# Attention scores issued two query tiles ahead, and a head's value products in two runs instead of four

## The chip, the cores and the metric

The kernel runs on one core of one Trainium2 chip. The metric is device time in microseconds (us) of one execution. The engines named below are TensorE (PE in the profile, with its weight loads as PEld), VectorE (DVE), ScalarE (ACT), GpSimd (POOL) and SyncE (SP), which issues most DMAs. Each works through its own queue in order; semaphores hold an instruction until what it needs is there.

## The reference

Three stages follow one another. The change touches only the first, an attention in which a query sees only the keys of its own hash bucket; its output goes through a routed mixture of experts and a gated feed-forward block.

```python
q_bits = (np.einsum('bhsd,dk->bhsk', q, proj) > 0); k_bits likewise   # 6 bits: a bucket
mask = q_bucket[:, :, :, None] == k_bucket[:, :, None, :]
scores = scale * np.matmul(q, k.transpose(0, 1, 3, 2))                # 2 x 8 heads, 768 x 768, head size 64
scores = np.where(mask, scores, -1000000000.0)
scores = scores - np.max(scores, axis=-1, keepdims=True)
attn = np.exp(scores)
attn = attn / (np.sum(attn, axis=-1, keepdims=True) + 1e-09)
return np.matmul(attn, v)
```

## The kernel before

The attention stage handles 16 heads (2 batches of 8) one after another, and each head in 6 query tiles of 128 rows. One loop over g counts all 96 tiles: head h = g // 6, tile t = g % 6. In this text "t0" to "t5" are the six passes of that loop for one head. A pass does this for its tile:

- `scores(g)` (L151): four matmuls on PE, two with 76 rows (64 of the head, 12 of the hash code) and two with the low parts of the split operands, into one of two buffers in PSUM (`ps_s`, `bufs=2`).
- `smax(g)` (L161): DVE reduces the 768 scores of each row (`mm`, L164), then a tiny scalar_tensor_tensor with two operands in SBUF makes scale and bias (`sb`, L165).
- `sexp(g)` (L170): ACT takes the exponential of the PSUM scores into `p`, with the row sum (L172, a second small instruction reads the accumulator).
- `tposes(g, half)` (L178): three PE transposes of 128x128 (L185) per half, each half then copied from PSUM by ACT (L189) or DVE (L191) into `PT`.

Other work is placed between these. For the head before, `av_step(h - 1, k)` (L195) makes the value product of key tile k with stationary operands 64 columns wide, two side by side (L200). For two heads before, `o_evac` and `o_out` (L217, L228) copy, scale and project the result. For the next head, `hash_mm(h + 1)` (L123, stationary operands 32 columns wide) and `hash_codes` (L140) make the hash code on DVE, and four small SP DMAs write it into the operands of the scores (L147). For the head after that, `split_a` (L100, ACT) and `split_b` (L107) split queries and keys into high and low parts: the query's low part on DVE (L115) beside a POOL copy (L116), the key's low part and copy both on POOL (L118, L119). `load(h + 3)` starts the input DMAs.

Everything is written out by hand (`tc.manual_schedule()`): each engine executes in the order in which the Python calls come. Before the change, pass g issues the scores of tile g + 1, then the value products or hash (list `early`), then the transposes of tile g, while the place of the exponential of tile g + 1 among the PSUM copies is set per pass by `K['se']`. `side(pos)` (L733) issues the exponential and the splits before, between and after the two halves of the transposes. `AV_AT` says which value products stand in which pass.

Of the kernel before, what the change touches and what calls it, by code (L numbers as in the profile page):

```python
# [21 lines left out]
N, DM, E, FF, F2 = 1536, 512, 8, 1024, 1536  # L22
C = 224
GR = ((0, 6), (6, 4), (10, 2))
K = {'se': (0, 1, 2, 1, 1, 2), 'ev': (0, 0, 0, 1, 0, 1, 0, 0, 0, 1, 0, 0), 'avl': (), 'oul': 0, 'hml': 0, 'hc': ((0, 0), (0, 2), (1, 1), (2, 1)), 'sa': ((2, 2), (4, 1)), 'sb': ((3, 2), (4, 2)), 'ext': (1, 0, 2, 4, 7, 8), 'hm0': 0, 'hc0': ((1, 0), (1, 2), (3, 0), (4, 1))}
C_ID, C_TRI, C_THR, C_REV, C_TOK, C_IOTA, C_BASE, C_SLOT = 0, 128, 256, 258, 266, 278, 279, 287
CW = C_SLOT + C
FAR = 1024.0
AV_AT = {1: (0, 1), 2: (2,), 3: (3, 4), 5: (5,)}


@with_exitstack
def attn_moe_kernel(ctx: ExitStack, tc: tile.TileContext, xin, cst, projd, wblk, wmoe, w2in, out):
# [54 lines left out]
    NHD = NB * NH  # L88
# [34 lines left out]
    def hash_mm(h, order=range(4)):  # L123
        p = (ps_m if h or 2 in order else ps_a).tile([128, 512], F32, tag="m" if h or 2 in order else "a", name="m")
        for j in order:
            i = j // 2
            hp_[h, j] = p
            PE.matmul(
                p[32 * j:32 * j + 32, :384], pst[:, 32 * i:32 * i + 32], X[h][:, j * 384:(j + 1) * 384],
                start=True, stop=True, skip_group_check=True,  # L130
            )
# [19 lines left out]
    def scores(g):  # L151
        h, t = divmod(g, NT)
        p = ps_s.tile([128, 2, 512], F32, tag="s", name="s")
        st[g] = p
        qs = slice(t * 128, t * 128 + 128)
        for c in range(2):
            sl = slice(c * 384, c * 384 + 384)
            PE.matmul(p[:, c, :384], T[h, 0][:76, qs], T[h, 1][:76, sl], start=True, stop=False)  # L158
            PE.matmul(p[:, c, :384], B[h, 0][:, qs], B[h, 1][:, sl], start=False, stop=True)  # L159

    def smax(g):  # L161
        m = mm[:, g % 4]
        sb = sm.tile([128, 2], F32, tag="sb", name="sb")
        DVE.tensor_reduce(out=m[:, 1:2], in_=st[g][:, :, :384], axis=AX.XY, op=ALU.min)  # L164
        DVE.scalar_tensor_tensor(  # L165
            out=sb, in0=m[:, 1:2].to_broadcast([128, 2]), scalar=BIG / 2, in1=m, op0=ALU.is_le, op1=ALU.mult
        )
        scl[g], nbs[g] = sb[:, 0:1], sb[:, 1:2]
# [26 lines left out]
    def av_step(h, k):  # L195
        if k == 0:
            av[h] = ps_a.tile([128, 512], F32, tag="a", name="av")
        v = V[h][:, k]
        for c in range(2):
            PE.matmul(  # L200
                av[h][c * 64:(c + 1) * 64, :384], v, PT[h][:, k, c * 384:(c + 1) * 384],
                start=(k == 0), stop=(k == NT - 1), skip_group_check=True,
            )
# [13 lines left out]
    def o_evac(h, q=None, copy=DVE.tensor_copy):  # L217
        n = q[1] * 128 if q else 384
        o = sm.tile([128, n], F32, tag="o" if q is None else f"o{n}", name="o", bufs=2 if q is None else 1)
        copy(o, av.pop((h, q) if q else h)[:, :n])  # L220
        oT[h, q] = o
        t0, nt = q or (0, NT)
        r = sm.tile([128, NT], F32, tag="r", name="r", bufs=2)
        DVE.tensor_reduce(out=r[:, :nt], in_=sums[:, h * 6 + t0:h * 6 + t0 + nt], axis=AX.X, op=ALU.add)
        DVE.reciprocal(r[:, :nt], r[:, :nt])
        rs[h, q] = r

    def o_out(h, q=None):  # L228
        b, hh = divmod(h, NH)
        o, r = oT.pop((h, q)), rs.pop((h, q))  # L230
        p = ps_m.tile([128, 512], F32, tag="m", name="m")
        t0, nt = q or (0, NT)
        t = slice(b * 6 + t0, b * 6 + t0 + nt)
        lp = sm.tile([128, nt, 16], F32, tag=f"lp{nt}", name="lp", bufs=2) if hh else lg[:, t]
        xo = x_all[:, t, hh * 64:(hh + 1) * 64]
        if q is None:
            for j in range(3):
                PE.matmul(p[:, j * 160:(j + 1) * 160], o[:, j * 128:(j + 1) * 128], wb[:, hh], start=True, stop=True)
            ps = p[:, :480].rearrange("p (j c n) -> p j c n", j=3, c=2)
            rr = r.rearrange("p (c j) -> p j c", c=2).unsqueeze(3)  # L240
            lo, xo, sh = lp.rearrange("p (c j) n -> p j c n", c=2), xo.rearrange("p (c j) n -> p j c n", c=2), [128, 3, 2]
        else:
            for j in range(nt):
                PE.matmul(p[:, j * 80:(j + 1) * 80], o[:, j * 128:(j + 1) * 128], wl, start=True, stop=True)
            ps = p[:, :nt * 80].rearrange("p (j n) -> p j n", j=nt)
            rr, lo, sh = r[:, :nt].unsqueeze(2), lp, [128, nt]
        DVE.tensor_tensor(out=lo, in0=ps[..., 64:], in1=rr.to_broadcast(sh + [16]), op=ALU.mult)
        DVE.tensor_tensor(out=xo, in0=ps[..., :64], in1=rr.to_broadcast(sh + [64]), op=ALU.mult)
        if hh:
            (DVE if hh >= NH - 2 else POOL).tensor_tensor(out=lg[:, t], in0=lg[:, t], in1=lp, op=ALU.add)  # L250
# [344 lines left out]
    with tc.manual_schedule():  # L595
# [72 lines left out]
        L = NHD - 1  # L668
# [6 lines left out]
        qa, qb = (0, 4), (4, 2)  # L675
        for g in range(NG):
            h, t = divmod(g, NT)
            if t == 1 and h + 3 < NHD:
                load(h + 3)
            if g + 1 < NG:  # L680
                scores(g + 1)
                smax(g + 1)
            if g < NT:
                set_up(g)
            if 2 * NT <= g < 2 * NT + (E * C + N) // 256:
                for i in (g - 2 * NT,):
                    nc.sync.dma_start(
                        out=xr[i * 256:(i + 1) * 256].rearrange("(p r) d -> p r d", p=128),
                        in_=zeros[0].unsqueeze(1).to_broadcast([128, 2, 512]),
                    )  # L690
            if g == 6 * NT:
                for n in range(4):
                    for part in range(2):
                        w_load(n, part)
            if g == 10 * NT + 1:
                r = router(0)
                todo = [r["s1"], r["s1b"], None, lambda: (r["s2"](), r["s2c"]()), r["s2b"], r["s4"], r["s4b"]]
                for f in r["sc"]:
                    todo += [f, None]
                todo += [r["s4c"], r["s3"], r["s5"]]  # L700
            early, late = [], []
            if h < L:
                if h:
                    for k in AV_AT.get(t, ()):
                        early.append(lambda k=k: av_step(h - 1, k))
                if h > 1 and t == 4:
                    (late if K["oul"] else early).append(lambda: o_out(h - 2))
                if t == (0 if h else K["hm0"]):
                    (late if K["hml"] else early).append(lambda: hash_mm(h + 1))
            elif t < 3:  # L710
                av_step(h - 1, 2 * t)
                av_step(h - 1, 2 * t + 1)
                if t == 0:
                    o_out(h - 2)
                if t == 2:
                    o_evac(h - 1)
            elif t == 3:
                o_out(h - 1)
            else:
                k = 3 * (t - 4)  # L720
                av_group(h, qa, (k, k + 1, k + 2))
                if t == 5:
                    o_evac(h, qa)
            for f in early:
                f()
            if h and h < L and t == 5 and not K["avl"].count(5):
                o_evac(h - 1)
            if g > 10 * NT + 1 and todo:
                f = todo.pop(0)
                if f:  # L730
                    f()

            def side(pos):  # L733
                if g + 1 < NG and K["se"][t] == pos:
                    sexp(g + 1)
                for i in range(2):
                    if h + 2 < NHD and K["sa"][i] == (t, pos):
                        split_a(h + 2, i)
                    if h + 2 < NHD and K["sb"][i] == (t, pos):
                        split_b(h + 2, i)  # L740
                if h < L and (t, pos) == (1, 0):
                    hash_codes(h + 1)

            side(0)
            tposes(g, 0)
            side(1)
            tposes(g, 1)
            for f in late:
                f()
            if h and h < L and t == 5 and K["avl"].count(5):  # L750
                o_evac(h - 1)
            side(2)
            for f in extra.get((h - L + 1, t), ()):
                f()
# [578 lines left out]
```

## Time and profile before

| | before |
|---|---|
| median of 3 runs | 748.94 us (748.5 to 750.65) |
| the profiled execution's own time | 749.55 us |
| its span, first to last instruction | 747.7 us |
| PE busy | 728.7 us (97%) |
| DVE busy | 527.3 us (71%) |
| ACT busy | 434.4 us (58%) |
| POOL busy | 279.4 us (37%) |
| granted PE clock | full speed over nearly the whole span |

The busy shares are means over all three stages. The attention stage takes roughly the first 260 us of the span. PE time is modelled at the end of each matmul, so successive matmuls overlap in the records; the start times tell the pace.

### The profile page before, as it was taken

The numbers are of one execution on the slowest core, as the hardware profiler recorded it, in microseconds if no ns is written. First come the engines' busy times: TensorE is split into PE (matmuls) and PEld (weight loads), VectorE is DVE, ScalarE is ACT, GpSimd is POOL, SyncE is SP. The second block draws the span as 40 slices with busy tenths as digits, with TensorE's granted clock in tenths as the row PEclk, the third lists the DMA queues.
The fourth block names the chain that finished last, engine by engine and source line by source line (L and its number), as shares of the span: only waits on it lengthen the run. The fifth ranks groups of instructions, "written<-read, shape, count | busy, mean of one in ns | idle before, by whom it ended". The sixth has DMA issues, their size and how long they took to land.

```text
span 747.7 us, 13437 instructions
## 1 busy us (share of the span) xinstructions
PE 728.7 (97%) x4621; PEld 617.5 (83%) x4622; DVE 527.3 (71%) x1033; ACT 434.4 (58%) x945; POOL 279.4 (37%) x319
## 2 busy tenths in 40 slices
PE   8899999999999999999999999999999999999995
PEld 6666666666666699999999999999999988999984
DVE  6787777778787777778779876778676245756641
ACT  6777777777777546666677744444554334344331
POOL 3222232322434265122111123444434466565543
PEclk9999999999999999999999999999999999999998
DMA  7367251221302038788897754545463332212202
GB/s 237 116 225 262 77 172 58 71 98 61 114 33 61 15 110 287 225 192 235 267 339 227 221 159 151 219 162 215 165 214 116 111 101 69 85 47 81 58 1 88
DMA packets 49594, 107.37 MB, mean 144 GB/s; under 512 B 8096, under 2 KB 11504, under 8 KB 47984
## 3 DMA queue, kind: packets, MB, share of 16 engines
q1 hardware_dynamic: 46848, 99.94, 41.4%
q0 software_dynamic: 2304, 6.31, 2.3%
q8 instruction: 38, 0.62, 0.4%
q14 instruction: 36, 0.29, 0.1%
q10 hardware_dynamic: 368, 0.20, 0.1%
HBM read 82.76 MB, written 22.56 MB: 141 GB/s over the span
## 4 chain that ended last, share of the span: by engine, by line
PE 80%; DVE 8%; ACT 5%; issue 4%; POOL 1%; DMA 1%; SPq 0%; DVEq 0%; POOLq 0%; ACTq 0%
PE tp L185 8%; PE av L200 8%; PE y L934 5%; PE acc L1056 4%; PE acc L1055 4%; PE acc L1057 4%; PE h L896 3%; PE h L895 3%; PE h L894 3%; PE s L158 3%; PE s L159 3%; ACT p L172 3%; PE y L935 3%; DVE mm L164 2%; PE abb L894 2%
## 5 line engine op out<-in xcount | busy, mean ns | idle before, releaser
L164 DVE TENSOR_REDUCE mm<-s 128x1 f32<-128x768 f32 x96 | 91.8, 956 | 31.5 <-PE s L159 27.1
L185 PEld LDWEIGHTS tp<-cs,p 128*128 128x128 f32 x576 | 62.1, 140 | 55.3 <-ACT p L172 35.9
L853 POOL TENSOR_TENSOR pc<-t,pc 128x256 fp32r<-128x256 f32 x86 | 74.8, 893 | 84.1 <-ACT pc L852 84.1
L172 ACT ACTIVATE p<-s,sb 128x768 f32<-128x768 f32 x96 | 95.0, 989 | 15.9 <-PE tp L185 8.9
L189 ACT ACTIVATE pt<-tp 128x384 f32<-128x384 f32 x144 | 67.0, 489 | 45.5 <-PE tp L185 44.3
L185 PE MATMUL tp<-cs,p 128*128 128x128 f32 x576 | 83.4, 281 | 6.8 <-ACT p L172 5.1
L478 DVE TENSOR_TENSOR wl<-wr,wh 128x512 fp32r<-128x512 f32 x125 | 81.0, 688 | 8.3 <-ACT wh L477 3.5
L477 ACT ACTIVATE wh<-wr 128x512 fp32r<-128x512 f32 x128 | 73.7, 624 | 4.0 <-DMA wr<-wmoe 3.9
L934 PE MATMUL y<-hl,wh 128*128 128x448 f32 x224 | 74.9, 378 | 0.2
L158 PE MATMUL s<-tk,tq 76*128 76x384 f32 x192 | 73.1, 381 | 0.3 <-DVE tq L135 0.3
L894 PE MATMUL h<-xh,wh 128*128 128x224 f32 x256 | 71.4, 279 | 0.2 <-ACT xh L411 0.2
L200 PE MATMUL av<-pt,v 128*64 128x384 f32 x360 | 71.1, 503 | 0.0
L896 PE MATMUL h<-xh,wl 128*128 128x224 f32 x256 | 70.6, 276 | 0.2 <-DVE wl L478 0.2
L895 PE MATMUL h<-xl,wh 128*128 128x224 f32 x256 | 70.2, 274 | 0.3 <-DVE xl L412 0.3
L159 PE MATMUL s<-bk,bq 128*128 128x384 f32 x192 | 65.0, 339 | 0.0
L935 PE MATMUL y<-hl,wl 128*128 128x224 f32 x224 | 59.5, 266 | 0.0
L1055 PE MATMUL acc<-h,gh 128*128 128x512 f32 x144 | 56.7, 394 | 0.4 <-ACT gh L1041 0.4
L1056 PE MATMUL acc<-l,gh 128*128 128x512 f32 x144 | 56.8, 395 | 0.0
L1057 PE MATMUL acc<-h,gl 128*128 128x512 f32 x144 | 56.7, 394 | 0.0
L865 POOL TENSOR_TENSOR l<-t,h 128x512 fp32r<-128x512 f32 x24 | 31.0, 1292 | 64.7 <-ACT h L864 64.7
L116 POOL CAST bq<-tq 64x768 fp32r<-64x768 f32 x15 | 19.3, 1288 | 89.3 <-ACT tq L103 87.4
L907 ACT ACTIVATE hl<-h 128x224 fp32r<-128x224 f32 x64 | 22.8, 356 | 47.6 <-PE h L896 46.8
(225 smaller groups left out, 1889.9 us busy)
## 6 DMA issues: line engine op xcount, KB each, us to landing
wr<-wmoe SPq DMA_DIRECT2D x128, 256.0 KB
r<-w2in SPq DMA_DIRECT2D x12, 1536.0 KB
x<-xin SPq DMA_DIRECT2D x30, 384.0 KB
w<-t SPq DMA_DIRECT2D x36, 256.0 KB
t<-w SPq DMA_DIRECT2D x36, 256.0 KB
xr<-zero SPq DMA_DIRECT2D x13, 512.0 KB
xg<-xr SPq DMA_DIRECT2D x14, 256.0 KB
v<-xin SPq DMA_DIRECT2D x16, 192.0 KB
```

The source lines that it names most:

```text
L158: PE.matmul(p[:, c, :384], T[h, 0][:76, qs], T[h, 1][:76, sl], start=True, stop=False)
L159: PE.matmul(p[:, c, :384], B[h, 0][:, qs], B[h, 1][:, sl], start=False, stop=True)
L164: DVE.tensor_reduce(out=m[:, 1:2], in_=st[g][:, :, :384], axis=AX.XY, op=ALU.min)
L172: ACT.activation(p.rearrange("p (c n) -> p c n", c=2), st.pop(g)[:, :, :384], ACTF.Exp, scale=scl.pop(g), bias=nbs.pop(g), accum_out=sums[ ...
L185: PE.transpose(ps[:, j * 128:(j + 1) * 128], pt_[g][:, k * 128:(k + 1) * 128], ident)
L200: PE.matmul(av[h][c * 64:(c + 1) * 64, :384], v, PT[h][:, k, c * 384:(c + 1) * 384], start=(k == 0), stop=(k == NT - 1), skip_group_check= ...
L894: PE.matmul(ps, wh, xh, start=first, stop=False)
L895: PE.matmul(ps, wh, xl, start=False, stop=False)
L896: PE.matmul(ps, wl, xh, start=False, stop=last)
L934: PE.matmul(p, wh[:, w], hl, start=(f == 0), stop=False, skip_group_check=True)
L1055: PE.matmul(acc[i], h[:, w], wh, start=(f == 0), stop=False)
L1056: PE.matmul(acc[i], h[:, w], wl, start=False, stop=False)
```

## The change

Three things change in the attention loop. Pass g issues the scores of tile g + 2 instead of g + 1 (the first pass issues both). The exponential of tile g + 1 always comes first on ACT, before the PSUM copies of the pass. The value products of a head stand in two runs of three key tiles, after the transposes of t1 and t4 (list `late`), instead of four runs of two, one, two and one before the transposes of t1, t2, t3 and t5. With them move the hash (t0 to t1, now behind the transposes and directly ahead of a run of value products), `o_out` (t4 to t3), `o_evac` (t5 to t4), the input load (t1 to t2) and the splits of queries and keys, for heads from the second on: ACT parts after t1 and t4, DVE and POOL parts after t2 and t5.

```diff
-K = {'se': (0, 1, 2, 1, 1, 2), ..., 'sa': ((2, 2), (4, 1)), 'sb': ((3, 2), (4, 2)), ..., 'hm0': 0, ...}
+K = {'se': (0, 0, 0, 0, 0, 0), ..., 'sa': ((1, 2), (4, 2)), 'sb': ((2, 2), (5, 2)), 'sa0': ((2, 2), (4, 1)), 'sb0': ((3, 2), (4, 2)), ...}
...
-AV_AT = {1: (0, 1), 2: (2,), 3: (3, 4), 5: (5,)}
+AV_AT = {1: (0, 1, 2), 4: (3, 4, 5)}
...
-            if t == 1 and h + 3 < NHD:
+            if t == 2 and h + 3 < NHD:
                 load(h + 3)
-            if g + 1 < NG:
-                scores(g + 1)
-                smax(g + 1)
+            for k in (g + 1, g + 2) if g == 0 else (g + 2,):
+                if k < NG:
+                    scores(k)
+                    smax(k)
...
             if h < L:
+                if t == (1 if h else 0):
+                    (late if h else early).append(lambda: hash_mm(h + 1))
+                    if h:
+                        late.append(lambda: hash_codes(h + 1))
                 if h:
                     for k in AV_AT.get(t, ()):
-                        early.append(lambda k=k: av_step(h - 1, k))
-                if h > 1 and t == 4:
-                    (late if K["oul"] else early).append(lambda: o_out(h - 2))
-                if t == (0 if h else K["hm0"]):
-                    (late if K["hml"] else early).append(lambda: hash_mm(h + 1))
-            elif t < 3:
-                av_step(h - 1, 2 * t)
-                av_step(h - 1, 2 * t + 1)
+                        late.append(lambda k=k: av_step(h - 1, k))
+                if h > 1 and t == 3:
+                    early.append(lambda: o_out(h - 2))
+            elif t < 2:
                 if t == 0:
                     o_out(h - 2)
-                if t == 2:
-                    o_evac(h - 1)
+                for k in range(3 * t, 3 * t + 3):
+                    late.append(lambda k=k: av_step(h - 1, k))
+                if t:
+                    late.append(lambda: o_evac(h - 1))
             elif t == 3:
                 o_out(h - 1)
-            else:
+            if h == L and t > 3:
                 k = 3 * (t - 4)
-                av_group(h, qa, (k, k + 1, k + 2))
+                late.append(lambda: av_group(h, qa, (k, k + 1, k + 2)))
                 if t == 5:
-                    o_evac(h, qa)
+                    late.append(lambda: o_evac(h, qa))
+            if h and t == 4 and h < L:
+                late.append(lambda: o_evac(h - 1))
             for f in early:
                 f()
-            if h and h < L and t == 5 and not K["avl"].count(5):
-                o_evac(h - 1)
...
-                    if h + 2 < NHD and K["sa"][i] == (t, pos):
+                    if h + 2 < NHD and K["sa" if h else "sa0"][i] == (t, pos):
                         split_a(h + 2, i)
-                    if h + 2 < NHD and K["sb"][i] == (t, pos):
+                    if h + 2 < NHD and K["sb" if h else "sb0"][i] == (t, pos):
                         split_b(h + 2, i)
-                if h < L and (t, pos) == (1, 0):
+                if (g, pos) == (1, 0):
                     hash_codes(h + 1)
```

## Rows read from the trace of the kernel before

**Rows 1.** Busy time by stretch: us, PE, PEld, DVE, ACT, POOL; PEclk, DMA share, GB/s.

```profile
100.00:125.00 25.00, 24.76 (x163) 15.79 (x161) 18.41 (x36) 18.61 (x38) 7.26 (x6) 1.00 0.34 119
...
110.00:111.00 1.00, 1.00 (x10) 0.92 (x9) 0.89 (x1) 0.34 (x1) 1.00 (x1) 1.00 0.00 0
```

**Rows 2.** Timeline of PE, one head (t0 to t5): start us, us, engine, line, tile.

```profile
100.01 0.42 PE L158 MATMUL s<-tk,tq 76*128 76x384 f32 x1
...
100.89 0.85 PE L128 MATMUL m<-x,pst 128*32 128x384 f32 x8
...
101.86 0.88 PE L185 MATMUL tp<-cs,p 128*128 128x128 f32 x6
...
102.50 0.42 PE L158 MATMUL s<-tk,tq 76*128 76x384 f32 x1
...
103.38 1.51 PE L200 MATMUL av<-pt,v 128*64 128x384 f32 x8
...
104.82 0.88 PE L185 MATMUL tp<-cs,p 128*128 128x128 f32 x6
...
105.45 0.42 PE L158 MATMUL s<-tk,tq 76*128 76x384 f32 x1
...
107.76 0.42 PE L158 MATMUL s<-tk,tq 76*128 76x384 f32 x1
...
110.71 0.42 PE L158 MATMUL s<-tk,tq 76*128 76x384 f32 x1
...
111.50 0.98 PE L238 MATMUL m<-wb,o 128*128 128x160 f32 x6
...
112.89 0.42 PE L158 MATMUL s<-tk,tq 76*128 76x384 f32 x1
...
115.21 0.42 PE L158 MATMUL s<-tk,tq 76*128 76x384 f32 x1
```

**Rows 3.** Timeline of PE, last head: value products directly behind transposes.

```profile
253.05 0.88 PE L185 MATMUL tp<-cs,p 128*128 128x128 f32 x6
253.85 1.93 PE L210 MATMUL av<-pt,v 128*64 128x512 f32 x6
```

**Rows 4.** Timeline of DVE and ACT: from scores to exponential.

```profile
100.72 0.99 ACT L172 ACTIVATE p<-s,sb 128x768 f32<-128x768 f32 x1
...
101.00 0.96 DVE L164 TENSOR_REDUCE mm<-s 128x1 f32<-128x768 f32 x1 [0.39 <-PE s L159]
...
117.18 0.20 DVE L165 SCALAR_TENSOR_TENSOR sb<-mm 128x2 f32<-128x2 f32 x1
...
117.50 0.99 ACT L172 ACTIVATE p<-s,sb 128x768 f32<-128x768 f32 x1 [0.50 <-DVE sb L165]
```

**Rows 5.** Timeline of POOL, DVE and ACT around the key splits.

```profile
99.00 0.84 ACT L103 ACTIVATE tk<-x 128x768 fp32r<-128x768 f32 x1
...
99.98 1.83 POOL L118 TENSOR_TENSOR bk<-x,tk 64x768 fp32r<-64x768 f32 x1 [1.60 <-issue]
...
101.86 0.82 POOL L119 CAST bk<-tk 64x768 fp32r<-64x768 f32 x1
101.99 0.71 DVE L165 SCALAR_TENSOR_TENSOR sb<-mm 128x2 f32<-128x2 f32 x1
```

**Rows 6.** Timeline of ACT and DVE: the copies, the query's low part, an undisturbed sb.

```profile
103.80 0.86 ACT L189 ACTIVATE pt<-tp 128x384 f32<-128x384 f32 x2
...
109.81 0.16 DVE L165 SCALAR_TENSOR_TENSOR sb<-mm 128x2 f32<-128x2 f32 x1
109.94 0.95 DVE L115 SCALAR_TENSOR_TENSOR bq<-x,tq 64x768 fp32r<-64x768 f32 x1
...
113.41 0.55 DVE L191 COPY pt<-tp 128x384 f32<-128x384 f32 x1
```

**Rows 7.** Timeline of SP: the last two DMAs of a hash code.

```profile
107.37 1.47 SPq L147 DMA_DIRECT2D tk<-code  x2
```

**Rows 8.** Waits of PE from 30 to 250 us: us in all, times, longest.

```profile
PE tp L185 <- ACT p L172: 1.5, 2, 1.0
```

More of the change, by code (lines that the diff above doesn't have):

```diff
@@ L24 @@
 GR = ((0, 6), (6, 4), (10, 2))
-K = {'se': (0, 1, 2, 1, 1, 2), 'ev': (0, 0, 0, 1, 0, 1, 0, 0, 0, 1, 0, 0), 'avl': (), 'oul': 0, 'hml': 0, 'hc': ((0, 0), (0, 2), (1, 1), (2, 1)), 'sa': ((2, 2), (4, 1)), 'sb': ((3, 2), (4, 2)), 'ext': (1, 0, 2, 4, 7, 8), 'hm0': 0, 'hc0': ((1, 0), (1, 2), (3, 0), (4, 1))}
+K = {'se': (0, 0, 0, 0, 0, 0), 'ev': (0, 0, 0, 1, 0, 1, 0, 0, 0, 1, 0, 0), 'hc': ((0, 0), (0, 2), (1, 1), (2, 1)), 'sa': ((1, 2), (4, 2)), 'sb': ((2, 2), (5, 2)), 'sa0': ((2, 2), (4, 1)), 'sb0': ((3, 2), (4, 2)), 'ext': (1, 0, 2, 4, 7, 8), 'hc0': ((1, 0), (1, 2), (3, 0), (4, 1))}
 C_ID, C_TRI, C_THR, C_REV, C_TOK, C_IOTA, C_BASE, C_SLOT = 0, 128, 256, 258, 266, 278, 279, 287
@@ L749, in attn_moe_kernel @@
                 f()
-            if h and h < L and t == 5 and K["avl"].count(5):
-                o_evac(h - 1)
             side(2)
```

## Prediction, made before the changed kernel ran

> **What bounds the kernel now.** I read the busy time by stretch first. In the attention stage PE is busy 24.76 of 25 us at full clock, while DVE, ACT and POOL have 6 us or more to spare [rows 1]. The list of waits says the same: over 220 us PE waited 1.5 us, in two places [rows 8]. So before the change a head costs what PE's instructions cost one behind the other. The timeline of PE gives that cost: from the first score matmul of t0 to that of the next head it is 115.21 - 100.01 = 15.20 us [rows 2]. This pace is regular, so I work out one head before, one head after, and multiply.
>
> **PE after the change, without waits.** The pass with `o_out` takes 112.89 - 110.71 = 2.18. From its first matmul at 111.50 to the next scores it is 1.39; the transposes take some .58 of that (105.45 - 104.82 = .63 in another pass, a twentieth of it for coming out of narrow products), so `o_out` takes .81 and a plain pass of scores and transposes 1.37. A pass with two value products of a key tile takes 105.45 - 102.50 = 2.95, with one 107.76 - 105.45 = 2.31 [rows 2]. The difference, .64, is one key tile; 2.31 - .64 - 1.37 = .30 is left, which every run of narrow products (64 columns) pays for going in and coming out. Four runs now, two after: -.60 a head. Coming from transposes instead of scores costs no more: in the last head value products start .80 after the first of six transposes [rows 3], of which the transposes themselves fill about .6, as in the 105.45 - 104.82 = .63 from transposes to scores.
>
> The pass with the hash takes 2.49, that is 1.12 over plain [rows 2]. About .19 of it is a wait for the exponential: this starts at 100.72 [rows 4], the transposes at 101.86, 1.14 later and .12 behind the end of the hash (100.89 + .85), while behind value products they start .07 ahead of the end (103.38 + 1.51 against 104.82). The exponential comes a pass earlier after the change, so that wait goes, and the hash costs .93. Put against a run of value products it shares one way in or out; I take .10 for it (0 to .20).
>
> A head without waits: t0, t2 and t5 plain 4.11, t3 with `o_out` 2.18, t4 1.37 + .30 + 3 x .64 = 3.59, t1 1.37 + .93 + .30 + 1.92 - .10 = 4.42. Sum 14.30, or .90 less than now.
>
> **The new wait.** The scores have two PSUM buffers. Now that they run two tiles ahead, scores g + 2 need the buffer that exponential g reads. From a first score matmul to the maximum it is .99 (100.01 to 101.00), from there to sb .99 (to 101.99), from sb to the exponential .28 (sb's own .16, and .12 from its end, as 117.18 + .20 to 117.50), and from the exponential until PE may go on 1.14: 3.40 [rows 2, 4 to 6]. Two passes of PE lie between. For t0 and t1, t1 and t2, t3 and t4, t4 and t5 they take 4.9 or more; for t2 and t3 3.55, just enough. For t5 and t0 they take 2.74. So the scores in t1 wait .66 in every head, and behind them in PE's queue stand the transposes, the hash and the value products. Nothing hides this: PE has no other instruction to turn to. Bounds: .60 to .75, as the maximum may also stand behind `o_evac` on DVE, which begins when the value products of t4 end and lasts about .8.
>
> **What the moved key split does to it.** Before the change the sb of t0 took .71 instead of .16: it started at 101.99, POOL's copy L119 ran from 101.86 to 102.68, and sb ended at 102.70 [rows 5, 6]. Now it costs nothing, since PE has the hash and value products to do. After the change the ACT part of the key split stands at the end of t4 and the POOL part behind it, so I ask what POOL does when the sb on the path, that of t5, is due. Counted from start to start (.08 less than the durations; two copies of .49 take .86 together): from the scores of t2 to the maximum .99, to sb .99, to the copy on DVE .08, to the query's low part .48, to the maximum of t3 .88, to its sb .99, to the exponential .28, to the copy on ACT .97, to the key split .43, to POOL's L118 .98 (99.00 to 99.98) [rows 4 to 6]. That is 7.07 after the scores of t2. On PE the scores of t5 come 1.37 + 2.18 + 3.59 = 7.14 after them. So L118 starts with the scores of t5, within about .1, and takes 1.83; L119 runs from 1.8 to 2.6. The sb is due at 1.98: inside L119, as now, and it ends with it, at 2.62 instead of 2.14. The exponential and the scores of t1 come .46 later (0 to .65 by the phase). The wait is then 1.12, and a head 14.30 + 1.12 = 15.42.
>
> The Trainium skill (SBUF — State Buffer, Who interferes with whom) speaks against this placement: a VectorE instruction with two SBUF inputs and a GpSimd instruction that reads SBUF exclude each other for a whole instruction, and the later one blocks fully. The trace agrees, with the .71 that ended with L119 [rows 5]; if the two only shared bandwidth, sb would lose a few hundredths and the total would be that of the second case below.
>
> **The other edits.** The hash code is on its way later. It is made in t1 about 5.0 after the scores of t0, its four DMAs leave by 8.8, and PE's first scores of the next head, now in t4, come at 1.37 + 4.42 + 1.12 + 1.37 + 2.18 = 10.46. Before, the last issue ended at 108.84 and the DMA engines were quiet from 110.00 on [rows 1, 7], so landing takes at most 1.2: hidden, by .5; if it came a microsecond late that would be .5 a head. In SP's queue the input load now stands behind these DMAs, with a whole head to land. Exponential first on ACT costs nothing: PE doesn't need the copies until a pass later, behind at least .72 of scores. The router's pieces (heads 10 to 14) still delay an exponential, for which PE now waits 1.0 once [rows 8]; I leave that. The first head does an extra score group before its first transposes: +.5 (0 to 1). The last head's tile order saves one run, .3, and two POOL splits in head 14 may now hold an sb that matters: nothing in sum (-.3 to +.7).
>
> **Sum.** 14 heads x -.90 = -12.6; 13 passages from one of them to the next x 1.12 = +14.6, first head +.5, and about .5 for the same wait, shorter, in t1 of head 1: +3.0. The profiled execution took 749.55 (span 747.7 and 1.85 around it), so 752.6; the median of the runs lies .6 below that execution: 752.0.
>
> **The rivals.** (1) *sb and POOL miss each other.* A phase of L118 .2 later, or .6 earlier, is enough, for instance if my chain of ten starts is off by a fiftieth each. Then only .66 is waited: -12.6 + 13 x .66 + 1.0 = -3.0, 746.0. For it: the margin is small. Against it: both ends of the phase hang on the same scores of t2. (2) *No wait at all*, as the fewer runs alone would give: -12.6 + .5, 736.8. It would need the path of 3.40 to shrink to 2.74; the rows leave no .66 to find. (3) *The second pair slips too.* t2 and t3 clear 3.40 by .15 only, with the query low part and `o_out`'s two DVE instructions beside them; .4 more a head is +5, 757. For it: DVE works almost without a break from t2 to t5. Against it: each piece has its place in the count above.
>
> **How the numbers follow.** Chances: forecast .55, (1) .25, (2) .06, (3) .14. What a measurement can tell from no change is .3%, 2.25 us. The forecast's own spread of 1.7 lies across 751.2: two thirds slower, one third the same. Case (1) is faster in seven of ten. So faster .24, same .24, slower .52. The range takes the forecast, most of (1) and the near part of (3): 744.5 to 756.5; the forecast's own is 750 to 754.5.
>
> **What would show it.** In the profile after: runs of value products of three key tiles and PE idle about 1.1 us ahead of the scores of t1, released by the exponential; a head of 15.4; sb of t5 near .6 to .7 long and ending with L119. A head near 14.95 with sb at .16 is rival (1); idle ahead of the scores of t4 as well is (3). I am wrong altogether if narrow products pay their .30 somewhere else, or if the scores don't wait for the exponential's buffer.

## The result, and the profile after

The changed kernel takes 756.85 us (median of 4 runs, 756.72 to 757.09) beside 749.74 for the kernel before on the same chip: ratio 1.0094, interval 1.0081 to 1.0108. It is slower, as forecast, but by 7.1 us where the forecast had 3, and it lies .35 above the top of the range. The profiled execution took 756.84.

The page's busy table and the list of waits of PE, first from 30 to 260 us, then over the whole span (us in all, times, longest):

```profile
span 755.1 us, 13379 instructions
...
PE 727.3 (96%) x4621; PEld 630.9 (84%) x4622; DVE 518.5 (69%) x1033; ACT 434.7 (58%) x945; POOL 273.0 (36%) x319
```

```profile
PE s L158 <- ACT p L172: 10.2, 15, 1.1
...
PE s L158 <- ACT p L172: 12.1, 16, 1.9
PE s L158 <- DMA tk<-code: 1.2, 1, 1.2
```

[rows 8] had two waits of transposes. Now there are fifteen of scores, one in nearly every head, all for an exponential: the new wait is there. The whole span has two more, of 1.9 and 1.2 us, both in the first head.

To see where 755.1 - 747.7 = 7.4 us went, I set the starts of the scores at each pass side by side. These are the first scores and the scores that open the t0 pass of head 1, before and after:

```profile
9.54 0.45 PE L158 MATMUL s<-tk,tq 76*128 76x384 f32 x1 [0.30 <-DVE tq L135]
...
24.09 0.42 PE L158 MATMUL s<-tk,tq 76*128 76x384 f32 x1
```

```profile
8.79 0.44 PE L158 MATMUL s<-tk,tq 76*128 76x384 f32 x1 [0.30 <-DVE tq L135]
...
28.66 0.42 PE L158 MATMUL s<-tk,tq 76*128 76x384 f32 x1
```

One more group of scores (.72) is done by then in the changed kernel, so 24.81 is the fair number for before, and 28.66 - 24.81 = 3.85 were lost. But the first scores stand .75 earlier in this profile, and that isn't the change: over the profiles of all runs they start anywhere from 8.57 to 9.77, also in kernels that are the same up to there. Counted from its first scores the first head takes 15.27 before and 19.87 after: it lost 4.60. Heads 1 to 14 take 214.31 before and 217.35 after.

| part of the span | forecast | measured |
|---|---|---|
| start of the first scores | 0 | -.75 |
| first head from there | +.5 | +4.6 |
| heads 1 to 12 | +2.0 | +1.7 |
| heads 13 and 14, with the router | +.4 | +1.4 |
| last head and what follows | 0 | +.5 |

**A steady head.** Where t5 of one head passes into t0 and t1 of the next, the timeline of the changed kernel reads (start us, us, engine, line, tile):

```profile
87.74 1.82 POOL L118 TENSOR_TENSOR bk<-x,tk 64x768 fp32r<-64x768 f32 x1 [1.72 <-issue]
87.88 0.45 PE L158 MATMUL s<-tk,tq 76*128 76x384 f32 x1
...
89.27 0.42 PE L158 MATMUL s<-tk,tq 76*128 76x384 f32 x1
...
89.62 0.82 POOL L119 CAST bk<-tk 64x768 fp32r<-64x768 f32 x1
...
89.96 0.50 DVE L165 SCALAR_TENSOR_TENSOR sb<-mm 128x2 f32<-128x2 f32 x1
...
90.56 0.99 ACT L172 ACTIVATE p<-s,sb 128x768 f32<-128x768 f32 x1 [0.46 <-DVE sb L165]
...
91.69 0.44 PE L158 MATMUL s<-tk,tq 76*128 76x384 f32 x1 [0.81 <-ACT p L172]
```

L118 starts .14 before the scores of t5 (forecast: within about .1). The sb starts 2.08 after those scores (forecast 1.98), in L119, and ends at 90.46 with it, at 90.44; undisturbed it takes .16 [rows 6]. The exponential follows, and 1.13 after its start PE goes on (1.14 in the forecast). From scores to scores t0 takes 91.69 - 89.27 = 2.42 where a plain pass takes 1.38: a wait of 1.04, of which the list shows .81, as the modelled ends of the transposes cover the rest.

**The first head.** Busy time by stretch (us, PE, PEld, DVE, ACT, POOL, PEclk, DMA share, GB/s), and PE's timeline:

```profile
10.00:12.00 2.00, 0.47 (x3) 0.15 (x1) 1.97 (x3) 1.59 (x2) 0.83 (x1) 0.88 0.91 283
12.00:14.00 2.00, 1.61 (x8) 1.18 (x10) 0.18 (x2) 1.39 (x4) 1.43 (x2) 0.50 1.01 390
...
16.00:18.00 2.00, 2.00 (x9) 1.93 (x8) 0.34 (x1) 1.51 (x3) 0.17 (x1) 0.50 0.08 31
...
22.00:24.00 2.00, 0.68 (x6) 0.36 (x4) 1.90 (x4) 2.00 (x5) 0.67 (x1) 1.00 0.09 18
...
26.00:28.00 2.00, 2.00 (x9) 1.90 (x8) 1.16 (x4) 2.00 (x4) 0.79 (x1) 0.50 0.82 320
```

```profile
12.39 0.69 PE L158 MATMUL s<-tk,tq 76*128 76x384 f32 x1 [1.92 <-ACT p L172]
...
13.97 1.51 PE L128 MATMUL m<-x,pst 128*32 128x384 f32 x8
15.41 1.54 PE L185 MATMUL tp<-cs,p 128*128 128x128 f32 x6
...
23.98 0.42 PE L158 MATMUL s<-tk,tq 76*128 76x384 f32 x1 [1.17 <-DMA tk<-code]
```

The third group of scores now stands ahead of the hash and waits 1.92 for exponential 0. Behind that idle time the granted clock is at the lower of its two levels (1.2 GHz, PEclk 0.50), with PE busy throughout: the hash takes 1.51 instead of .85 [rows 2], six transposes 1.54 instead of .88. The hash code is made at 19.34 instead of 15.83, the scores that need it wait for its DMA, PE is idle again (.68 busy of 2), and the clock falls a second time. Before, PE waited for no code in the first head, and the clock stayed at 1.00 from 10 to 16 us, though PE was busy for only .88 us of 12 to 14:

```profile
12.00:14.00 2.00, 0.88 (x9) 0.87 (x8) 1.79 (x3) 2.00 (x4) 0.68 (x2) 1.00 0.98 368
```

### The profile page after: what moved, and what is told of

It is laid out like the page before. It is cut to its first block, busy times and chain, and to the rows that moved or that the text cites. A ratio compares the mean times of both kernels' runs of the same rounds, so it can differ in the third digit from the quotient of the medians.

```text
span 755.1 us, 13379 instructions
## 1 busy us (share of the span) xinstructions
PE 727.3 (96%) x4621; PEld 630.9 (84%) x4622; DVE 518.5 (69%) x1033; ACT 434.7 (58%) x945; POOL 273.0 (36%) x319
## 4 chain that ended last, share of the span: by engine, by line
PE 83%; DVE 6%; issue 3%; ACT 3%; POOL 2%; DMA 1%; SPq 0%; ACTq 0%; DVEq 0%; POOLq 0%
PE av L200 8%; PE y L935 6%; PE tp L185 6%; PE s L158 5%; PE acc L1057 4%; PE acc L1056 4%; PE acc L1058 4%; PE s L159 4%; PE h L897 4%; PE h L896 3%; PE h L895 3%; PE y L936 3%; PE abb L895 2%; ACT p L172 2%; PE aba L896 2%
## 5 line engine op out<-in xcount | busy, mean ns | idle before, releaser
L158 PE MATMUL s<-tk,tq 76*128 76x384 f32 x192 | 76.0, 396 | 13.7 <-ACT p L172 12.1
L185 PEld LDWEIGHTS tp<-cs,p 128*128 128x128 f32 x576 | 70.8, 144 | 7.5 <-issue 2.0
L158 PEld LDWEIGHTS s<-tk,tq 76*128 76x128 f32 x192 | 37.6, 196 | 36.4 <-ACT p L172 24.5
L159 PE MATMUL s<-bk,bq 128*128 128x384 f32 x192 | 67.1, 349 | 0.0
L200 PE MATMUL av<-pt,v 128*64 128x384 f32 x360 | 64.7, 494 | 0.0
L200 PEld LDWEIGHTS av<-pt,v 128*64 128x64 f32 x360 | 23.2, 136 | 32.9 <-issue 25.4
```

The costliest lines, as they stand in the source:

```text
L185: PE.transpose(ps[:, j * 128:(j + 1) * 128], pt_[g][:, k * 128:(k + 1) * 128], ident)
L200: PE.matmul(av[h][c * 64:(c + 1) * 64, :384], v, PT[h][:, k, c * 384:(c + 1) * 384], start=(k == 0), stop=(k == NT - 1), skip_group_check= ...
```

## The experiments

There are two theories. **F**, the first head: some 4 of the 7.1 us come from the third group of scores standing ahead of the hash, through the clock, through the order or both; the steady heads cost what was forecast. **The path**: the loss is made in the steady heads, where exponential and scores share two PSUM buffers and sb is held by POOL's key split. The rival to the path's second part is that sb only loses a little there, and that PE is short of work for another reason. The kernel before ran beside each experiment, at 750.31, 750.15 or 749.2 us.

**The first head in its old order** (`e1_first_head`). Pass 0 issues scores 1 alone, and scores 2 behind its transposes; the codes of head 1 go ahead of scores 3.

```diff
-            for k in (g + 1, g + 2) if g == 0 else (g + 2,):
-                if k < NG:
-                    scores(k)
-                    smax(k)
-            if g < NT:
+            if g == 1:
+                set_up(1)
+                hash_codes(1)
+            k = g + 1 if g == 0 else g + 2
+            if k < NG:
+                scores(k)
+                smax(k)
+            if g < NT and g != 1:
                 set_up(g)
...
+            if g == 0:
+                late += [lambda: scores(2), lambda: smax(2)]
...
-                if (g, pos) == (1, 0):
-                    hash_codes(h + 1)
```

> The changed kernel, but the first pass issues only the scores of tile 1 ahead of the hash and its transposes, those of tile 2 behind them, and the first hash code is made ahead of the scores of tile 3; all else as changed. Theory F (the miss of the forecast lies in the first head: PE stands behind the scores of tile 2, its clock falls to half, the first hash code comes late): 3 to 4 us come back, 753 to 754 us, and the granted clock stays full over the first 30 us. Rival H (the miss is spread over the heads, the first head only shifts work): under 1 us comes back, 756 to 757 us.

It took 752.41 (ratio 1.0031, 1.0017 to 1.0045), 2.1 above the kernel before beside it, where the changed kernel lies 7.1 above. Its stretches:

```profile
10.00:12.00 2.00, 1.92 (x15) 0.98 (x13) 1.91 (x4) 0.76 (x2) 0.70 (x1) 1.00 0.95 328
12.00:14.00 2.00, 0.94 (x8) 0.94 (x9) 1.72 (x3) 2.00 (x5) 0.76 (x2) 1.00 1.00 386
```

The clock stays at 1.00, and t0 of head 1 starts at 24.63, which is before's 24.81 less .18 (from the first scores 15.17, against 15.27). Heads 1 to 14 take 242.0 - 24.63 = 217.37, as in the changed kernel, though not head by head: head 12 is .5 longer here, heads 13 and 14 are .5 shorter. So the first head accounts for some 4 to 5 of the 7.1 us, and F holds.

**The new order, with PE kept busy** (`e2_heat`). Thirty small matmuls whose results nobody reads fill PE's wait ahead of scores 2.

```diff
                 if k < NG:
+                    if k == 2:
+                        heat(30)
                     scores(k)
```

> The changed kernel with 30 idle-filling matmuls of 128 columns ahead of the scores of tile 2 in the first pass; every wait stays where it is. If the half clock is what the first head costs (theory F, clock part), full clock through the first 25 us and 2 to 3 us back: 754 to 755 us. If the price is the wait itself and the late hash code (theory F, order part), the clock recovers but the time stays at 756 to 757 us.

```profile
10.44 1.85 PE L619 MATMUL warm<-ones 128*128 128x128 bf16 x30
12.51 0.45 PE L158 MATMUL s<-tk,tq 76*128 76x384 f32 x1 [0.22 <-ACT p L172]
...
13.42 0.85 PE L128 MATMUL m<-x,pst 128*32 128x384 f32 x8
...
21.54 0.42 PE L158 MATMUL s<-tk,tq 76*128 76x384 f32 x1 [1.17 <-DMA tk<-code]
...
25.45 0.44 PE L158 MATMUL s<-tk,tq 76*128 76x384 f32 x1 [0.35 <-ACT p L172]
```

754.0 (1.0056, 1.0037 to 1.0075). Scores 2 start as late as in the changed kernel (12.51 against 12.39), but the clock is at 1.00, the hash takes .85, and t0 of head 1 starts 12.94 later, at 25.45; in the changed kernel it starts 28.66 - 12.39 = 16.27 later. So the clock costs 3.3 us. The order by itself costs 1.3: from its first scores, at 8.92, the first head takes 16.53, against 15.27 before. Nearly all of that is the wait of 1.17 for the hash code, which is as long here at full clock as in the changed kernel, and which neither the kernel before nor `e1_first_head` has.

**The key split one stage earlier** (`e3_key_split`). Its second half moves from t4 and t5 to t2 and t3.

```diff
-'sa': ((1, 2), (4, 2)), 'sb': ((2, 2), (5, 2)),
+'sa': ((1, 2), (2, 2)), 'sb': ((2, 2), (3, 2)),
```

> The changed kernel with the key split moved: its ACT part after t2 instead of t4, its POOL part after t3 instead of t5. Theory of the lock (the sb of t5 waits for POOL's L119): that sb falls from about 0.6 to 0.16, the wait ahead of the scores of t1 from about 1.0 to 0.7, heads from 15.4 to 15.0, in all 3 to 5 us: 752 to 754 us. Rival (the sb is not on the path, the wait has another cause): heads stay at 15.4, 756 to 757 us.

758.07 (1.0097, 1.0066 to 1.0128): the expectation is missed. DVE and POOL in a steady head:

```profile
87.00 1.08 DVE L165 SCALAR_TENSOR_TENSOR sb<-mm 128x2 f32<-128x2 f32 x1
90.25 0.16 DVE L165 SCALAR_TENSOR_TENSOR sb<-mm 128x2 f32<-128x2 f32 x1
```

```profile
86.25 1.82 POOL L118 TENSOR_TENSOR bk<-x,tk 64x768 fp32r<-64x768 f32 x1
88.13 0.83 POOL L119 CAST bk<-tk 64x768 fp32r<-64x768 f32 x1
```

The sb that t0's exponential needs (90.25) is free, and t0 takes 2.17 instead of 2.42. But POOL now meets the sb before it, which lasts until L118 ends (88.08 and 88.07). Steady heads are only .2 faster (15.23 against 15.43), and head 13 takes 19.76, as the router's pieces meet the split. The lock moved; it did not go.

**The hash back in t0** (`e4_hash_t0`). The hash of the next head gives PE something to do between the scores in t0 and those in t1.

```diff
-                if t == (1 if h else 0):
+                if t == 0:
                     (late if h else early).append(lambda: hash_mm(h + 1))
```

> The changed kernel with the hash matmuls and the hash code back in t0, behind its transposes; value products stay in t1 and t4. Theory of the path (scores, maximum, sb, exponential, scores take 3.4 us and two plain passes of PE only 2.7): t5 and t0 now give PE 3.7 us of work, so the wait ahead of the scores of t1 shrinks to 0 to 0.2, a head from 15.4 to 14.4 to 14.6, and the time by 10 to 13 us to 744 to 747 us. Rival (the wait is fixed by something else, the buffer of the transposes or ACT's order): the wait stays near 1 us, the head at 15.4 to 15.5.

746.51 (.9941, .9917 to .9965). PE over t0 of a head:

```profile
98.09 0.42 PE L158 MATMUL s<-tk,tq 76*128 76x384 f32 x1
...
98.89 0.81 PE L185 MATMUL tp<-cs,p 128*128 128x128 f32 x6
99.64 0.85 PE L128 MATMUL m<-x,pst 128*32 128x384 f32 x8
100.50 0.45 PE L158 MATMUL s<-tk,tq 76*128 76x384 f32 x1
```

t0 still takes 2.41, now with the hash in it, and t1 falls from 4.43 to 3.65; a head takes 14.65 instead of 15.43. t1 is .78 shorter in every head. t0, with the hash now in it, is as long as it was in most heads, .25 longer in the three where it took 2.08 (heads 2, 7 and 12), and shorter in head 6. One edit that adds and removes no instruction does this, so PE was idle there waiting and not slow: the path holds. The first head is that of the changed kernel, instruction for instruction; in the profiled execution (742.53) scores 2 waited as long, 1.91, and yet the clock stayed at 1.00, and t0 of head 1 came 12.94 after scores 2 instead of 16.27. The other executions took 743.65 and 746.28 to 747.56. They have no trace, but their mean granted clock is on record: .998 for the two shortest, .991 to .995 for the four others (.989 to .995 in the four of the changed kernel). So the gap, near 3.3, goes with the clock, and 746.51 is a median over both kinds.

**Both together** (`e7_all`): the edits of `e1_first_head` and `e4_hash_t0`.

> The changed kernel with the first pass of e1_first_head and the hash of e4_hash_t0. If the two causes are separate they add up: first head 11 us instead of 16.3, heads 14.6 instead of 15.4: 740 to 743 us. If the gain of e4_hash_t0 came partly from the clock in the first head, which these runs share, 744 to 747 us.

743.24 (.9917, .9892 to .9942). Head 1 starts at 24.77, steady heads take 14.57 to 14.64: the first head of the one experiment and the heads of the other. In the profile the two causes add up, and the time is 6.9 below the kernel before beside it (just above what was expected).

**Scores two ahead without the rest** (`e5_ahead_only`): the kernel before, with scores two tiles ahead (pass 0 as in `e1_first_head`) and the exponential first; four runs of value products ahead of the transposes, the hash in t0, as before.

```diff
-            if g + 1 < NG:
-                scores(g + 1)
-                smax(g + 1)
+            k = g + 1 if g == 0 else g + 2
+            if k < NG:
+                scores(k)
+                smax(k)
...
-'se': (0, 1, 2, 1, 1, 2)
+'se': (0, 0, 0, 0, 0, 0)
```

> The kernel before with one part of the change alone: scores two tiles ahead and exponential first on ACT (the first pass as in e1_first_head); value products stay in four runs ahead of the transposes, hash in t0, splits where they were. Theory of the path: every two neighbouring passes hold 4.5 us of PE work or more, so no wait for the PSUM buffer; the head loses only the wait of 0.2 in t0, 15.0 us, and the time is 746 to 749 us. Rival (the second PSUM buffer makes PE wait in any order): heads of 15.5 or more, over 753 us.

751.18 (1.0011, .9994 to 1.0028): no change that can be told, where a gain was expected. The steady heads do take 15.00, .19 less than before, and the scores wait there for their buffer only once, for .2. That is given back elsewhere: head 1 starts 26.61 - 24.81 = 1.8 later, behind a wait for the code in the first head, and head 13 takes 17.38 instead of 16.26.

```profile
22.48 0.41 PE L158 MATMUL s<-tk,tq 76*128 76x384 f32 x1 [1.80 <-DMA tk<-code]
```

**Two runs without scores two ahead** (`e6_one_ahead`).

```diff
-            for k in (g + 1, g + 2) if g == 0 else (g + 2,):
-                if k < NG:
-                    scores(k)
-                    smax(k)
+            if g + 1 < NG:
+                scores(g + 1)
+                smax(g + 1)
```

> The changed kernel with the scores back at one tile ahead; value products in two runs, exponential first. Theory: in the plain passes the transposes now stand only one group of scores and one of transposes behind the scores that they need, 1.4 us against a path of 3.4, so each of the four plain or nearly plain passes waits 1 to 2 us: heads of 18 to 21 us, 790 to 840 us in all. Rival (the runs alone pay, being two ahead is what costs): heads of 14.5 to 15, 745 us or less.

One execution: 813.05, as expected; heads of 18.2 to 20.5 in the first eight. The plain passes no longer cover the way from scores to copied probabilities (waits of PE over the whole span):

```profile
PE tp L185 <- ACT pt L189: 42.8, 33, 2.2
PE tp L185 <- ACT p L172: 9.2, 19, 1.1
```

So the two runs can't be had without the scores two ahead, with the exponential first on ACT as here. Most of the wait is for ACT's copies, which stand behind that exponential; the old places of the exponential with two runs were not tried.

**Six runs instead of two** (`e9_six_runs`): `e7_all` with one key tile of value products in each pass.

```diff
-AV_AT = {1: (0, 1, 2), 4: (3, 4, 5)}
+AV_AT = {t: (t,) for t in range(6)}
...
-            if h and t == 4 and h < L:
+            if h and t == 5 and h < L:
                 late.append(lambda: o_evac(h - 1))
```

> e7_all (743.2 us) with the value products in six runs of one key tile, one at the end of every pass, instead of two runs of three. Theory that each run of narrow products pays 0.3 us for going in and out: four more runs (the hash shares one) cost 1.0 to 1.2 us a head, less the wait of 0.3 ahead of the scores of t1 that the filled passes hide: heads 15.3 to 15.6, 753 to 758 us. Rival (the runs cost nothing, all is waits): heads of 14.4, 740 to 742 us.

757.58 (1.0113, 1.0091 to 1.0135), steady heads 15.74 against 14.64. There is no wait of PE between 30 and 220 us, so the 1.10, and the .07 that `e7_all` waits in t0 (2.40 against the 2.33 of `e13_best`, which has no wait there), are the price of four more runs: .29 for each, as a mean. The run that follows the hash costs less than the others, as the hash is made of narrow products too: with .64 for a key tile, t0 takes 3.14, which is 2.33 (with the hash alone) + .64 + .17, and a plain pass with a run by itself 2.36, which is 1.38 + .64 + .34.

**POOL's key split late** (`e11_pool_late`): `e1_first_head` with POOL's second piece in t2 of the next head. The key's low part is then made from rows over which the hash code has been written, so this kernel's scores are other numbers.

```diff
-                    if h + 2 < NHD and K["sb" if h else "sb0"][i] == (t, pos):
+                    if h + 2 < NHD and K["sb" if h else "sb0"][i] == (t, pos) and not (h and i):
                         split_b(h + 2, i)
...
+                if 1 < h < L and (t, pos) == (2, 2):
+                    split_b(h + 1, 1)
```

> e1_first_head (752.4 us) with POOL's part of the key split moved into t2 of the next head, behind the copy of the query split; ACT's part stays. Theory of the lock: no POOL instruction runs when the sb of t5 is due, it takes 0.16 in every head, all heads are 15.0 to 15.1 us like the ones that already escape, and 2.5 to 3.5 us go: 749 to 750 us. Rival (the longer heads have another cause): heads stay at 15.4, 752 to 753 us.

790.63 (1.0562): far off what was expected, since the place was badly chosen; scores of the next head wait for the split in t4 (6.1 to 8.4 instead of 3.63), and the clock falls six times in the first 280 us. What it does show is t0 at 2.08 in heads 2 to 13 (1.85 in head 11), with POOL's pieces away from it.

**The whole key split at the end of t0** (`e10_split_t0`): `e1_first_head`, with this from head 2 on.

```diff
-'sa': ((1, 2), (4, 2)), 'sb': ((2, 2), (5, 2)),
+'sa': ((1, 2), (0, 2)), 'sb': ((2, 2), (0, 2)), 'sa1': ((1, 2), (4, 2)), 'sb1': ((2, 2), (5, 2)),
```

> e1_first_head (752.4 us) with the whole key split, ACT's and POOL's part, moved to the end of t0 for heads from the second on, well before the hash code of that head; POOL then works in t1, where PE has 4.4 us of its own. Theory of the lock: the sb of t5 is 0.16 in every head, t0 takes 2.08 in all of them as in the heads that escape now, heads 15.1 instead of 15.4: 749 to 750.5 us. Rival (the longer heads have another cause): t0 stays at 2.4 in most heads, 752 to 753 us.

754.93 (1.0079, 1.0059 to 1.0099): missed. DVE and POOL of a head:

```profile
88.00 0.16 DVE L165 SCALAR_TENSOR_TENSOR sb<-mm 128x2 f32<-128x2 f32 x1
90.09 1.34 DVE L165 SCALAR_TENSOR_TENSOR sb<-mm 128x2 f32<-128x2 f32 x1
91.82 0.66 DVE L142 TENSOR_SCALAR code<-m,thr 128x384 fp32r<-128x384 f32 x1
```

```profile
89.59 1.82 POOL L118 TENSOR_TENSOR bk<-x,tk 64x768 fp32r<-64x768 f32 x1 [7.55 <-ACT tk L103]
91.46 0.82 POOL L119 CAST bk<-tk 64x768 fp32r<-64x768 f32 x1
```

```profile
97.08 0.44 PE L158 MATMUL s<-tk,tq 76*128 76x384 f32 x1 [0.25 <-DMA tk<-code]
```

t0 is 2.08 in every head from 2 on (1.85 in head 11): with POOL away the sb takes .16, and only the wait for the buffer is left. But the next sb lasts 1.34, to the end of L118 (91.43 and 91.41), the hash code queues behind it on DVE, and the scores of the next head wait for the code; t3 and t4 grow to about 2.4 and 3.95 to 4.13, and a head takes 15.6 to 15.8.

**The best of these** (`e13_best`): `e7_all` with that key split, and one piece of the router (`s3`) behind the transposes.

```diff
-                    f()
+                    (late.append if len(todo) == 1 else lambda f: f())(f)
```

> e7_all (743.2 us) with the key split of e10_split_t0, and the router's two small exponentials in head 13 put behind the pass's own work instead of ahead of its exponential. Theory: sb on the path undisturbed, 0.1 us a head; the wait of 1.8 us in t4 and t5 of head 13 goes: 740 to 742 us. Rival: nothing more to gain, PE only waits elsewhere, 743 us or more.

741.56 (.9896, .9877 to .9915): about 1% below the kernel before, and clear of the noise. Steady heads take 14.57, each alike, instead of up to 14.64 in `e7_all`, and head 13 takes 15.86 instead of 16.36. By the times alone it can't be told from `e7_all`, as the two intervals overlap. PE from 25 to 235 us in this kernel, and in the changed one:

```profile
25.00:235.00 210.00, 208.04 (x1399) 151.07 (x1401) 170.79 (x337) 166.30 (x335) 63.48 (x66) 1.00 0.35 117
```

```profile
25.00:235.00 210.00, 199.33 (x1325) 145.31 (x1323) 154.01 (x319) 155.67 (x315) 58.43 (x61) 0.98 0.34 116
```

With the hash a pass earlier the code has time to land (PE does not wait for it from 30 to 220 us), so the split at the end of t0 costs nothing here, where it cost `e10_split_t0` half a microsecond a head.

## Why the prediction was off, step by step

**The step that failed** is the term "The first head does an extra score group before its first transposes: +.5 (0 to 1)". It counted the scores' own time and no more; from its first scores on, the first head lost 4.6. The term left out two things. PE stands idle 1.92 ahead of scores 2, so the hash behind them comes late, and the scores of head 1 wait 1.17 for its code: 1.3 in all, by `e2_heat` and `e4_hash_t0`, where the clock stayed up. And the clock is down afterwards: 3.3 us. The idle time could be read before, in the first head there:

```profile
11.15 0.85 PE L128 MATMUL m<-x,pst 128*32 128x384 f32 x8
...
12.00 0.99 ACT L172 ACTIVATE p<-s,sb 128x768 f32<-128x768 f32 x1 [1.14 <-DVE sb L165]
```

Exponential 0 starts at 12.00, PE may go on 1.14 later, and the hash, which fills this time at 11.15, now stands behind scores 2. The wait of a third group of scores for exponential 0 is the very wait that I worked out for t5 and t0; I did not put it into the first head. That the clock would fall as well could not be read there: it stayed at 1.00. With 4.6 for .5, the forecast of 752.0 would have been 756.1.

The first head in its old order, at 752.41, is about the kernel that I forecast, but that is in part luck: in its profile the first head, heads 1 to 12, heads 13 and 14 and the rest are off from the forecast by -.7, +.2, +.4 and +.5, which nearly cancel.

**PE without waits: right.** 14.30 was forecast. The plain passes take 1.38, t3 2.17, t4 3.63 (forecast 3.59) and t1 4.43 (4.42), in all 14.37. The .30 that a run of narrow products pays shows as .34 for a run by itself and .17 for one behind the hash (`e9_six_runs`). The Trainium skill (TensorEngine Tiling (Array Packing), Key Properties) says that changing the tiling mode drains TensorE; that fits, and it gives no price. The .19 wait that was to go with the exponential a pass earlier went: heads of 15.00 against 15.19 with two ahead alone.

**The wait for the PSUM buffer: right.** .66 was forecast (.60 to .75); without the lock it is 2.08 - 1.38 = .70. That it is a wait, `e4_hash_t0` shows: most of the hash vanishes into it.

**The lock: right in place, smaller in size.** .46 was forecast (0 to .65), about .33 came (t0 of 2.36 to 2.42 in seven heads, 2.58 and 2.69 in two, against 2.08), as sb is due .1 later in L119 than I had it. By the prediction's own numbers its .46 is 2.62 - 2.14 = .48, its chances give .26 for the same and .51 for slower, and the time without a lock would be that of its rival (1). The Trainium skill (SBUF — State Buffer, Who interferes with whom) has an exclusive lock; the trace agrees: sb ends within .02 us of L119 here, and of L118 in `e3_key_split` and `e10_split_t0`. In both of these the split was moved, and another sb paid.

**The rivals.** (1), sb and POOL missing each other, came in three heads, 2, 7 and 12, at 15.09 to 15.10; I gave it 14.95. (2), no wait, did not come. (3), the second pair slipping too, did not come either: t4 takes 3.63, with no idle ahead of its scores. So the total landed near (3)'s 757 for another reason.

**The router** was left out of the sum ("I leave that") and heads 13 and 14 cost 1 us over the forecast. In the changed kernel:

```profile
226.03 0.24 ACT L315 ACTIVATE rt_ed<-rt_d 128x48 f32<-128x48 f32 x1 [2.32 <-DVE rt_d L314]
...
226.50 0.97 ACT L172 ACTIVATE p<-s,sb 128x768 f32<-128x768 f32 x1
...
227.62 0.44 PE L158 MATMUL s<-tk,tq 76*128 76x384 f32 x1 [1.03 <-ACT p L172]
```

ACT stands 2.32 us behind an operand from DVE, the exponential queued behind it is late, and PE's scores wait 1.03. About half of that 1 us goes with the clock, which falls again behind this (PEclk 0.50 from 230 to 232 us): in `e1_first_head`, where it stays at 1.00 from 222 to 250 us, the two heads take 32.65 instead of 33.19. The cause of the .5 in the last head stays open.

## What to carry to other kernels

Issuing work further ahead moves a wait to the next shared buffer: work out the whole way from the producer to the release of that buffer, and put independent matmuls (here the hash) where the passes between are shorter. Work out the first iteration by itself, with the clock in the sum, since the pipeline isn't full there. A GpSimd instruction that locks out VectorE has to be placed where the small instruction that it holds has slack, and where what queues behind that has slack too.

## What the runs showed of the hardware

The same first head ran at either level of the clock. PE's idle time ahead of scores 2 was 1.92 us in the changed kernel, 1.91 in `e3_key_split` and 1.91 in `e4_hash_t0`. In the first two PEclk was 0.50 behind it (from 12 to 18 us, and from 14 to 18), in the third it stayed at 1.00. The wait of 1.17 for the code (1.16 in `e3_key_split`) is in these three and in `e2_heat`, and the clock fell behind it in the changed kernel alone. The stretches of `e4_hash_t0` behind the two waits:

```profile
12.00:14.00 2.00, 1.84 (x13) 0.97 (x14) 0.83 (x1) 1.17 (x4) 1.65 (x2) 1.00 1.04 398
...
22.00:24.00 2.00, 2.00 (x15) 1.87 (x15) 1.44 (x3) 1.15 (x3) 0.00 (x0) 1.00 0.90 343
```

The Trainium skill (TensorE: Matmul & The Clock Gate, What's actually happening) says of the ramp at a kernel's start that how much runs cold varies from run to run of one kernel, and that it costs under 1% of a typical span. Here the clock falls later, but the record agrees with both: the six executions of `e4_hash_t0` have mean clocks of .991 to .998, and 3.3 of 755.1 us is .4%. That is still nearly half of what this change cost, and what decides between the two levels is not shown here.
